# Later output stores, two-part first loads and an earlier column sum in an attention + MLP kernel

## The chip, the cores and the metric

The kernel runs on one core of a Trainium2 chip. The metric is device time in microseconds (us) of a whole execution, the median of several runs; less is better. A difference counts as faster or slower from 2% on, which would be 6.6 us here. One traced execution of each kernel gives its profile. The profile's span is about 1.7 us shorter than the device time, and single executions of one kernel spread over some 2 us.

## The reference

Eight batches of eight heads, 576 tokens of 64 values. Attention by landmarks (32 segment means of q and k), a pseudo-inverse by six Newton steps, then layer norm and a two-layer MLP with a residual.

```python
q_lm = q.reshape(B, H, m, S // m, D).mean(axis=3)          # m = 32 landmarks
k_lm = k.reshape(B, H, m, S // m, D).mean(axis=3)
A, Bm, C = sm(q, k_lm), sm(q_lm, k_lm), sm(q_lm, k)        # sm: scaled softmax(a b^T)
Z = Bm^T / (norm1(Bm) * norminf(Bm) + 1e-6)                # column and row sums of Bm
for _ in range(6):
    Z = 2 * Z - Z @ Bm @ Z
x = heads_side_by_side(A @ Z @ C @ v)                      # 8 x 576 x 512
out = x + relu(layernorm(x) * g @ w1) @ w2                 # 512 -> 2048 -> 512
```
(Written shorter than the original, with the same meaning.)

## The kernel before

PE is the busiest engine. The first batch's attention (a0) runs alone, with idle "warming" matmuls between its steps; afterwards the attention of later batches is interleaved with the MLP, whose matmuls come from a generator (`fill(n)` takes n steps of it). All loads, all DMA transposes of the normalized blocks (xn to xnT) and nearly all output stores are issued from one queue, that of SyncE. Loads of 576 KB feed six staging buffers; POOL casts them to fp16 and adds up segments.

The end of an MLP block, which issues its stores at once:

```python
ot = mout.tile([P, DM], FP32, name="ot", tag="ot")
dve.scalar_tensor_tensor(out=ot[:], in0=pso[:], scalar=rstds[g][:, u:u + 1],
                         in1=x_blk.pop(j)[:], op0=ALU.mult, op1=ALU.add)
store(j, ot)                      # two DMAs, one for each half block
yield True
```

A step of the interleaved part. `settle()` runs postponed work, among it POOL's centering of a block and its DMA transpose; `next_cast()` casts a landed load on POOL and issues a further load:

```python
for step, _ in enumerate(attention2(c.bs, c)):
    fill(count[step])
    settle()
    ...
        next_cast()
```

An MLP group needs four transposed blocks before its first matmul:

```python
while len(turned.get(g, ())) < 4:
    ...
```

The ramp, a0 (cut): the last k is cast whole, PE takes its segment sums (pss), then its nine transposes (pst); psb is bm's product, psse holds bm's self-product and its column sums, pscv the product with v.

```python
for _ in range(4):
    run(a0)
    warm(3, 256)
run(a0)
warm(1, 512)
run(a0)
scalar.copy(natv_buf[0][:, 3, :, 0:D], raw[0]["v", 1][:, 1])   # half of the second v on ACT
```

The softmax here doesn't subtract the row's maximum and nothing guards it: scores larger than these inputs give would overflow.

## Time and profile before

| | value | how to read it |
|---|---|---|
| time | 329.13 us, 3 runs (328.23 to 330.18); with three more runs 329.38 | device time |
| PE busy | 314.7 of 327.9 us | leaves 13.2 us, 3.9 us of them after the last matmul |
| PE idle, 0 to 26 us | 3.7 us | the ramp, beside warming matmuls |
| PE idle, 47 to 141.7 us | 4.8 us | small waits, and one of 1.42 us at its end |
| PE idle, 141.7 to 324 us | 0.1 us | nothing to gain here but work removed |

In the profile's lines PE is the matmul engine, PEld its weight load, SPq the queue of SyncE. A timeline line is: start, duration, engine, source line, operation, output<-input, and in brackets the idle time of the engine before it with what ended it. A line of the waits is: engine, tile, what it waited for: total, times, longest. A line of the chain that ended last is: start, duration, engine, tile. The lines themselves stand in the prediction. Idle times with two decimals in the text are summed from the trace's matmul records, gap by gap.

### The profile page before, as it was taken

The numbers are of one execution on the slowest core, as the hardware profiler recorded it, in microseconds if no ns is written. First come the engines' busy times: TensorE is split into PE (matmuls) and PEld (weight loads), VectorE is DVE, ScalarE is ACT, GpSimd is POOL, SyncE is SP. The second block draws the span as 40 slices with busy tenths as digits, with TensorE's granted clock in tenths as the row PEclk, the third lists the DMA queues.
The fourth block names the chain that finished last, engine by engine and source line by source line (L and its number), as shares of the span: only waits on it lengthen the run. The fifth ranks groups of instructions, "written<-read, shape, count | busy, mean of one in ns | idle before, by whom it ended". The sixth has DMA issues, their size and how long they took to land.

```text
span 327.9 us, 8249 instructions
## 1 busy us (share of the span) xinstructions
PE 314.7 (96%) x3409; PEld 162.3 (50%) x3409; DVE 175.7 (54%) x395; ACT 152.7 (47%) x307; POOL 153.3 (47%) x241
## 2 busy tenths in 40 slices
PE   8889999999999999989999999999999999999995
PEld 8547864553445444435544445454444444444444
DVE  3668769779964797953237668722566120010012
ACT  3546762749960661957204672454046107305600
POOL 3389979999999999999800034100014000000000
PEclk9999999999999999999999999999999999999998
DMA  7999999898797864695022103330242126032023
GB/s 278 394 356 365 366 402 303 297 345 239 241 195 231 234 169 127 156 290 102 4 68 66 34 20 76 82 50 2 64 104 26 32 64 98 0 72 60 0 49 79
DMA packets 36397, 50.34 MB, mean 154 GB/s; under 512 B 17796, under 2 KB 22152, under 8 KB 36360
## 3 DMA queue, kind: packets, MB, share of 16 engines
q1 hardware_dynamic: 36200, 49.69, 52.7%
q8 instruction: 26, 0.43, 0.5%
q10 hardware_dynamic: 160, 0.13, 0.2%
q14 instruction: 11, 0.09, 0.1%
HBM read 36.70 MB, written 9.44 MB: 141 GB/s over the span
## 4 chain that ended last, share of the span: by engine, by line
PE 56%; POOL 22%; DMA 7%; issue 2%; ACT 2%; DVE 1%; SPq 0%; POOLq 0%
PE psh L74 26%; PE pso L74 25%; POOL asum L68 11%; POOL nat L68 6%; POOL natv L68 3%; DMA stg<-in_q_dram 3%; POOL xn L68 2%; DMA w2stg<-in_moe_w_ch_dram 2%; POOL s L68 1%; PE psy L74 1%; PE pscv L74 1%; DMA stg<-in_v_dram 1%; DMA stg<-in_k_dram 1%; DMA xnT<-xn 1%; ACT xn L68 1%
## 5 line engine op out<-in xcount | busy, mean ns | idle before, releaser
L74 PE MATMUL psh<-xnT,w 128*128 128x512 f16 (+1 forms) x640 | 133.7, 358 | 1.4 <-DMA xnT<-xn 1.4
L74 PE MATMUL pso<-w,hT 128*128 128x512 f16 (+1 forms) x592 | 132.9, 374 | 0.0
L68 ACT ACTIVATE hT<-psh 128x512 f16<-128x512 f32 x144 | 84.9, 597 | 97.6 <-PE psh L74 97.4
L74 PEld LDWEIGHTS <-w 128*128 128x128 f16 x640 | 59.5, 98 | 56.7 <-issue 3.1
L74 PEld LDWEIGHTS <-hT 128*128 128x128 f16 x592 | 56.1, 98 | 57.2 <-issue 0.8
L68 DVE SCALAR_TENSOR_TENSOR ot<-pso,rstd,xblk 128x512 f32<-128x512 f32 (+1 forms) x37 | 27.1, 732 | 77.6 <-PE pso L74 77.4
L68 POOL CAST nat<-stg 128x1152 f16<-128x1152 f32 x28 | 32.5, 1167 | 3.4 <-DMA stg<-in_k_dram 1.7
L68 POOL TENSOR_TENSOR asum<-asum 128x256 f32<-128x256 f32 (+2 forms) x54 | 28.4, 527 | 4.2
L68 DVE TENSOR_TENSOR xblk<-psy,rcpd 128x512 f32<-128x512 f32 (+1 forms) x40 | 27.6, 691 | 1.8 <-POOL w L68 0.2
L68 POOL TENSOR_TENSOR asum<-nat 128x576 f32<-128x576 f16 x18 | 23.4, 1299 | 1.5
L68 POOL TENSOR_SCALAR xn<-xblk,mvg 128x512 f16<-128x512 f32 x14 | 9.6, 694 | 30.9 <-ACT junk L68 30.9
L68 DVE SCALAR_TENSOR_TENSOR st<-st,psn 128x192 f16<-128x192 f16 (+3 forms) x36 | 14.2, 395 | 17.6 <-PE psn L74 17.4
L68 POOL CAST natv<-stg 128x1152 f16<-128x1152 f32 (+1 forms) x16 | 17.6, 1119 | 9.6 <-DMA stg<-in_v_dram 9.6
L68 POOL TENSOR_SCALAR negm<-mvg 128x1 f32<-128x1 f32 x14 | 2.7, 191 | 40.5 <-DVE mvg L68 35.9
L68 DVE TENSOR_TENSOR ebd<-st,mask 128x256 f16<-128x256 f16 (+1 forms) x30 | 20.7, 690 | 1.0
L68 DVE STREAM_TRANSPOSE xT<-nat 128x576 uint32<-128x576 uint32 x24 | 18.2, 760 | 2.2 <-POOL nat L68 2.2
L74 PE MATMUL psy<-zcbd,ea 128*128 128x260 f16 (+1 forms) x80 | 15.9, 276 | 1.0 <-DVE xblk L68 0.4
L68 ACT ACTIVATE ea<-psea 128x576 f16<-128x576 f32 x12 | 7.2, 648 | 16.5 <-PE psea L74 16.5
L74 PE MATMUL idle<-zeros 128*128 128x128 f16 (+2 forms) x82 | 13.4, 312 | 1.1 <-DVE eps_ln L172 1.1
L74 PEld LDWEIGHTS <-ea 128*128 128x128 f16 (+1 forms) x80 | 7.1, 100 | 12.2 <-issue 3.5
L68 ACT ACTIVATE junk<-xblk 128x512 f16<-128x512 f32 x14 | 8.8, 625 | 9.4 <-DVE xblk L68 9.2
L68 DVE BATCH_NORM_STATS2 st<-xblk 128x6 f32<-128x512 f32 x18 | 12.4, 688 | 0.5
(115 smaller groups left out, 263.0 us busy)
## 6 DMA issues: line engine op xcount, KB each, us to landing
stg<-in_q_dram SPq DMA_DIRECT2D x16, 576.0 KB, 6.0
stg<-in_k_dram SPq DMA_DIRECT2D x16, 576.0 KB, 5.7
out_dram<-ot SPq DMA_DIRECT2D x70, 128.0 KB, 2.4
stg<-in_v_dram SPq DMA_DIRECT2D x10, 576.0 KB, 6.4
w1stg<-in_moe_w_ch_dram SPq DMA_DIRECT2D x16, 256.0 KB, 6.0
w2stg<-in_moe_w_ch_dram SPq DMA_DIRECT2D x16, 256.0 KB, 5.2
stg<-in_v_dram SPq DMA_DIRECT2D x12, 288.0 KB, 5.5
xnT<-xn SPq DMA_TRANSPOSE x28, 3.3
```

Of the source, the lines that this page charges most:

```text
L68: return lambda *args, **kw: keep(getattr(self.engine, op)(*args, **kw))
L74: keep(nc.tensor.matmul(o, l, r, start=start, stop=stop, tile_position=(rb, cb), skip_group_check=(skip or cb != 0)))
```

## The change

Three intents. Stores go into the queue one step later, so that loads and transposes of a step come ahead of stores whose data are older. The first batch's last k and last v arrive in two transfers each and are cast in two parts, so that work starts on the first part. The column sums of bm, which do not need bm's transpose, go ahead of bm's product with itself. Some warming matmuls go too. Core of the diff (cuts marked):

```diff
+    halves = ((slice(0, 2), slice(0, 5)), (slice(0, 2), slice(5, NJ)))
+    pairs = ((slice(0, 1), slice(0, NJ)), (slice(1, 2), slice(0, NJ)))
...
-            raw[b]["k", u] = load(k, b, u, nc.sync)
+            raw[b]["k", u] = load(k, b, u, nc.sync, halves if (b, u) == (0, U - 1) else whole)
...
-            raw[b]["v", u] = load(v, b, u, nc.sync)
+            raw[b]["v", u] = load(v, b, u, nc.sync, pairs if (b, u) == (0, U - 1) else whole)
...
+    pool.tensor_copy(out=natv_buf[0][:, 3, 5:NJ, 0:D], in_=raw[0]["v", 1][:, 1, 5:NJ])
...      (sums and transposes of that k: blocks 0 to 4, then 5 to 8; xT's first five by ACT, the rest by DVE)
+        MM(psse[:, 0, :, :], bones[:].rearrange("p a c -> p (a c)"), bm16[:])
         for w in range(W):
             for h in range(4):
                 sl = ds(32 * h, 32)
                 MM(psse[sl, 1, w, :], bmT[sl, w, :], bmT[sl, w, :], rb=32 * h, cb=32 * h)
-        MM(psse[:, 0, :, :], bones[:].rearrange("p a c -> p (a c)"), bm16[:])
...      (pscv of the last unit: v's first row of heads first, then its second)
-                store(j, ot)
+                if at_end:
+                    store(j, ot)
+                else:
+                    to_store.append((j, ot))
...
+    def work(n):
+        k = len(to_store)
+        fill(n)
+        settle()
+        for _ in range(k):
+            store(*to_store.pop(0))
...
-    for _ in range(4):
+    for i in range(4):
         run(a0)
-        warm(3, 256)
+        if i < 3:
+            warm(3, 256)
     run(a0)
-    warm(1, 512)
+    warm(1, 128)
     run(a0)
-    scalar.copy(natv_buf[0][:, 3, :, 0:D], raw[0]["v", 1][:, 1])
+    scalar.copy(natv_buf[0][:, 3, 0:5, 0:D], raw[0]["v", 1][:, 1, 0:5])
...
-            fill(count[step])
-            settle()
+            work(count[step])
```

More of the change, by code (lines that the diff above doesn't have):

```diff
@@ L78, in TR, with load @@
         keep(nc.tensor.matmul(o, i_, idn, is_transpose=True, tile_position=(0, 0)))
-    def load(src, b, u, queue):
+    whole = ((slice(0, 2), slice(0, NJ)),)
+    halves = ((slice(0, 2), slice(0, 5)), (slice(0, 2), slice(5, NJ)))
+    pairs = ((slice(0, 1), slice(0, NJ)), (slice(1, 2), slice(0, NJ)))
+    def load(src, b, u, queue, parts=whole):
         t = stage.tile([P, 2, NJ, D], FP32, name="stg", tag="stg")
-        keep(queue.dma_start(
-            out=t[:],
-            in_=src[b, 4 * u:4 * u + 4].rearrange("(r e) (t j) d -> (e t) r j d", e=2, j=NJ)))
+        rows = src[b, 4 * u:4 * u + 4].rearrange("(r e) (t j) d -> r (e t) j d", e=2, j=NJ)
+        for r, j in parts:
+            keep(queue.dma_start(out=t[:, r, j, :],
+                                 in_=rows[r][:, :, j, :].rearrange("r p j d -> p r j d")))
         return t
@@ L111, in cast_qk @@
         t = nat.tile([P, NJ, 2, D], FP16, name="nat", tag="nat")
-        engine.tensor_copy(out=t[:].rearrange("p j r d -> p r j d"), in_=raw[b][nm, u][:])
+        for _, j in halves if (b, u, nm) == (0, U - 1, "k") else whole:
+            engine.tensor_copy(out=t[:, j, :, :].rearrange("p j r d -> p r j d"),
+                               in_=raw[b][nm, u][:, :, j, :])
         nat_tiles[b, nm, u] = t
@@ L309, in attention, with sums @@
                 pst = p2([P, NJ, P], FP16, "pst")
-                def sums():
-                    for j in range(NJ):
+                def sums(js=range(NJ)):
+                    for j in js:
                         MM(pss[:, i, w, :], n16[:, j, :, :].rearrange("p r d -> p (r d)"),
@@ L316, in attention @@
                 last = (w, i) == (W - 1, 1)
-                if last:
+                if last and not first:
                     sums()
-                for j in range(NJ):
-                    TR(pst[:, j, :], n16[:, j, :, :].rearrange("p r d -> p (r d)"), ident16[:])
+                for js in (range(0, 5), range(5, NJ)) if first and last else (range(NJ),):
+                    if first and last:
+                        sums(js)
+                    for j in js:
+                        TR(pst[:, j, :], n16[:, j, :, :].rearrange("p r d -> p (r d)"),
+                           ident16[:])
                 t = aprep.tile([P, NJ, P], FP16, name="xT", tag="xT" + nm, bufs=5 if nm == "q" else 4)
@@ L325, in attention @@
                     scalar.copy(t[:], pst[:])
+                else:
+                    scalar.copy(t[:, 0:5, :], pst[:, 0:5, :])
                 xT[nm, w] = t
@@ L340, in attention @@
         if first:
-            dve.tensor_copy(out=t[:], in_=pst[:])
+            dve.tensor_copy(out=t[:, 5:NJ, :], in_=pst[:, 5:NJ, :])
         yield
@@ L401, in attention @@
             natv = natv_of[b]
-            for j in range(NJ):
-                for h in range(4):
-                    r, e = divmod(h, 2)
-                    rows = ds(64 * e, 64)
-                    MM(pscv[ds(32 * h, 32), w, :], ect[w][rows, j, ds(32 * r, 32)],
-                       natv[rows, 2 * u + r, j, :], rb=64 * e, cb=32 * h,
-                       start=(j == 0), stop=(j == NJ - 1), skip=True)
+            order = [(j, h) for j in range(NJ) for h in range(4)]
+            if first and w == W - 1:
+                order.sort(key=lambda jh: jh[1] // 2)
+            for j, h in order:
+                r, e = divmod(h, 2)
+                rows = ds(64 * e, 64)
+                MM(pscv[ds(32 * h, 32), w, :], ect[w][rows, j, ds(32 * r, 32)],
+                   natv[rows, 2 * u + r, j, :], rb=64 * e, cb=32 * h,
+                   start=(j == 0), stop=(j == NJ - 1), skip=True)
         rcv = asm.tile([P, W], FP32, name="rcv", tag="rcv")
@@ L940, in mlp @@
                                          in1=x_blk.pop(j)[:], op0=ALU.mult, op1=ALU.add)
-                store(j, ot)
+                if at_end:
+                    store(j, ot)
+                else:
+                    to_store.append((j, ot))
                 yield True
     stream = mlp()
+    to_store, at_end = [], []
     def fill(n):
@@ L1038 @@
     for i, _ in enumerate(a1):
-        fill(5 if i < 9 else 7)
-        settle()
+        work(5 if i < 9 else 7)
         next_cast()
@@ L1053 @@
         for step, _ in enumerate(attention2(c.bs, c)):
-            fill(count[step])
-            settle()
+            work(count[step])
             if late and step >= 3:
@@ L1063 @@
         while after and (after.jobs or after.lms):
-            fill(8)
+            work(8)
             next_cast()
             after.next_job()
+    at_end.append(True)
     for _ in stream:
-        pass
+        while to_store:
+            store(*to_store.pop(0))
 _INS = ['q', 'k', 'v', 'moe_g_ln', 'moe_w_ch1', 'moe_w_ch2']
```

## The prediction

> **What bounds the kernel now.** I read the views in this order: busy time by engine and the 40 slices, the chain that ended last, the waits of PE from the end of the ramp on, the SyncE queue around the largest of those waits, and the timeline of the first 16 us.
>
> ```profile
> PE 314.7 (96%) x3409; PEld 162.3 (50%) x3409; DVE 175.7 (54%) x395; ACT 152.7 (47%) x307; POOL 153.3 (47%) x241
> PE   8889999999999999989999999999999999999995
> POOL 3389979999999999999800034100014000000000
> DMA  7999999898797864695022103330242126032023
> ```
>
> PE is busy 96% of the span. Only 327.9 - 314.7 = 13.2 us are left, and 3.9 us of them are the tail after the last matmul. The slices show three more regimes: DMA full for the first six slices (to about 49 us), POOL full from about 33 to 141 us, and PE alone after that. The busy times by window say it in numbers: PE idles 3.7 us in 0 to 26 us (its 13.4 us of warming matmuls, tile idle, sit there too), 0.7 us in 26 to 47, 4.8 us in 47 to 141.7, and 0.1 us in 141.7 to 324. So after 141.7 us nothing but PE work matters, and the change removes no useful PE work. It can only bring forward the moment at which PE may run without stops.
>
> That moment is in the chain of waits and in PE's list of waits from 26 us on (engine, tile, releaser: total, times, longest):
>
> ```profile
> 136.22 2.16 POOL natv L68 x2
> 138.38 3.20 DMA xnT<-xn
> 141.71 1.89 PE psh L74 x8
> ...
> PE psn L74 <- DVE ebd L68: 1.6, 3, 0.7
> PE psh L74 <- DMA xnT<-xn: 1.4, 1, 1.4
> ```
>
> PE ran dry at 140.29 us and stood 1.42 us until the fourth transposed block of its next MLP group landed. The SyncE queue shows why that transpose was late:
>
> ```profile
> 133.82 1.22 SPq L870 DMA_TRANSPOSE xnT<-xn  x1
> 135.09 0.57 SPq L106 DMA_DIRECT2D stg<-in_q_dram  x1
> 135.75 1.20 SPq L870 DMA_TRANSPOSE xnT<-xn  x1
> 137.04 1.24 SPq L829 DMA_DIRECT2D out_dram<-ot  x2
> 138.38 1.25 SPq L870 DMA_TRANSPOSE xnT<-xn  x1
> ```
>
> POOL had finished that block's xn at 136.22 us (134.86 + 1.36), but the queue was issuing two output stores for 1.24 us and took the transpose at 138.38. The stores' data were ready at 133.75; they were ahead only by program order.
>
> In the ramp two waits matter:
>
> ```profile
> 11.63 0.12 PEld L74 LDWEIGHTS <-qbd 64*32 64x32 f16 x8 [0.32 <-DVE qbd L68]
> ...
> 13.49 0.68 ACT L68 CAST natv<-stg 128x576 f16<-128x576 f32 x1
> 13.52 0.67 POOL L68 CAST natv<-stg 128x576 f16<-128x576 f32 x1 [1.44 <-DMA stg<-in_v_dram]
> ...
> 14.24 0.47 PE L74 MATMUL pscv<-natv,ect 64*32 64x65 f16 x36 [0.31 <-POOL natv L68]
> ```
>
> bm's product (psb) starts 0.31 us after qbd is there (10.91 + 0.41), because four warming matmuls stand ahead of it; and the last pscv matmuls wait for the casts of the second v, which landed at 13.5 us.
>
> **What the Trainium skill says.** (1) "DMA: Bandwidth & Descriptors", section "Anatomy of one DMA": DMA engines do not wait on semaphores, the wait is on the issuing sequencer. So one queue is strictly in order, and a store ahead holds a transpose behind it. The five lines above agree. (2) The same page, "Why small descriptors are slow": a fixed cost for each packet. The packet records agree: 2304-byte packets took about 92 ns in the first 14 us, 1024-byte ones 48.6 ns in 20 to 28 us, so 18% more for each byte. (3) "Perfetto Trace Analysis", "DMA Optimizations": splitting may let work start sooner "if DMA engines are generally idle". Here they are not: their share in 10 to 26 us is about 1. (4) "TensorE: Matmul & The Clock Gate", Part 1: the array slows after an idle window of about 3.4 us. The granted clock is 1.00 up to 300 us, and the warming matmuls that go (three of 256 columns; 512 to 128 columns in another) leave a pause of well under 1 us, so I expect no loss.
>
> **The change part by part.**
>
> *Stores one step later.* The built order on SyncE shows what the scheduler made of it: ahead of the third of those transposes one half-block store is left instead of two (its partner moved to before the first). One store costs 1.24 / 2 = 0.62 us of issue. Walking the queue: transpose 1 at 133.82, load at 135.09, transpose 2 at 135.70, one store to 137.6, transpose 3 at about 137.6 instead of 138.38. It lands 3.3 us later, near 140.9, still later than PE's 140.29. Worth about 0.75 us, and at most the whole wait of 1.42 us. Other stores also move behind loads, but POOL waits for a load after 47 us only 1.2 us in all, all of it before 51 us, so this brings nothing there. After 141.7 us PE does not wait, so delayed stores cannot help or hurt; the four ot buffers cover one step (an ot comes about every 3.5 us).
>
> *k of the first batch's second half in two parts.* The last k lands at 9.38 us, its cast takes 0.76 us, PE's sums start at 10.22 and end at 10.65, klm starts at 10.70. A straight line through the two packet sizes gives (estimate) 57 ns for 1280 bytes; the two parts cost 57 + 49 = 106 ns where 92 did, on 16 packets for each engine: 0.22 us more, plus 0.03 for one more completion. So part 1 lands near 8.8, part 2 near 9.65. Casts (0.76 us for 1152 elements) shrink to about 0.49 and 0.43: done at 9.35 and 10.1. PE however is occupied with the third step's warming matmuls until about 9.8, then five sums, five transposes, four sums: klm at about 10.58, a gain of 0.1 us only. With the warming matmuls ahead of psb gone, psb starts on qbd's end, about 11.25 instead of 11.64. ACT takes xT's first five blocks at 10.54 to 11.25, before the exponential needs it at 11.5, so that split does not hurt.
>
> *Column sums ahead of bm's product.* They need bm (done at 12.84) and not bmT (13.12). With the 0.4 us from psb, the sums start near 12.5 instead of 13.33, so the DVE chain to st's first part ends near 13.65 instead of 14.47: 0.8 us.
>
> *v in two parts.* v has the same run length, so the cost is the 0.25 us inherited from k and one completion: the last part lands near 13.75. Its cast is now shared, 5 blocks on ACT (320 elements, about 0.48 us by the slope between 0.68 for 576 and 1.12 for 1152) and 4 on POOL (about 0.40): done at 14.25 instead of 14.20. Then 18 matmuls instead of 36 remain: about 0.31 instead of 0.47 us. rcv starts at 14.62 instead of 14.76.
>
> Sum of the ramp: v stays the last to arrive, the 0.8 us on the other branch is mostly slack, and the ramp's end moves by about **0.15 us**. Why v is so late: fifteen of its sixteen engines had finished by 12.37, one at 13.47, because a 16 KB instruction fetch (10.94 us, 1.07 us long) held that engine. If the fetch falls elsewhere, the ramp gains up to 0.8 us.
>
> Do these 0.15 us reach the end? Only if nothing with its own clock stands between. It does: DMA is full to about 47 us, then POOL runs one cast or sum after another to 138 us. POOL's chain starts when its first new k lands at 47.55 us, and DMA time sets that, not the ramp. So PE gains 0.15 us at 26 us and loses it again at 141.7. On the other hand the 0.25 us of dearer packets can push POOL's chain and the gate back by up to that much.
>
> Total: -0.75 from the queue, between 0 and +0.27 from the packets, some -0.1 from luck in the ramp: about -0.7 us on 329.13. I put the point a little lower, at 328.2, as each part removes a real wait, and the small waits of DVE ebd (1.6 us) may shrink with an earlier ramp.
>
> **Rivals.** (a) *The ramp is what counts*: PE is in truth its own bound from 26 us on, the 97% busy PE carries any ramp gain to the end, and the two gains add: 0.15 to 0.8 plus 0.75 to 1.4 us, so 327.0 to 328.2. For it: only 5.5 us of PE idle after 26 us, most of it waits for DVE that move along with PE. Against it: POOL's unbroken chain. (b) *The dearer packets win*: everything after 47 us comes 0.3 us later and the transposes gain little because the scheduler left one store ahead: 329.0 to 329.4. For it: the DMA share of 1. Against it: POOL has waited 0.9 us at 47.55, but in a DMA-bound stretch that is no slack. (c) *A new wait*: the moved stores hold up a later transpose or load, or an ot buffer, and PE stands after 141.7 us: up to 330. Against it: the transposes in the second half are issued well ahead, and PE waits for none of them.
>
> **Range and chances.** Main reading 328.0 to 328.7, rival (a) down to 327.0, rival (b) and run scatter (328.23 to 330.18 in three runs) up to 329.3. So **328.2 us, range 326.9 to 329.4**. A gain of 2% would be 6.6 us, half of all PE idle time: **faster 0.02, within 2% 0.97, slower 0.01**.
>
> **What would show it.** Right: PE's wait for xnT near 141 us shrinks from 1.4 to 0.3 to 0.9 us with the transpose issued about 137.6; psb near 11.25; the column-sum product starts before the bmT product near 12.5; rcv near 14.6; the first batch's last k in packets of 1280 and 1024 bytes; POOL's first new k still at 47.5 to 47.9 us. Wrong: if the PE wait at 141 us is gone and PE finishes over 1.2 us earlier, the ramp gain was carried (rival a); if POOL's chain moves earlier as a whole, DMA was not its clock; if PE's idle time after 142 us exceeds 0.5 us, rival (c) holds.

## The result, and the profile after

The changed kernel took 329.16 us (median of 6 runs, 328.16 to 329.51) beside 329.38 us (6 runs, 328.23 to 330.18) for the kernel before. A ratio here is the mean time of one kernel's runs over that of the other's of the same rounds, so it is not quite the ratio of the two medians. It was 0.9992, with a 95% interval of 0.9968 to 1.0016. Two later measurements of the same pair gave 0.9975 (0.9957 to 0.9994) and 0.9989 (0.9970 to 1.0009). The plain mean of the three is 0.9985, about -0.5 us. So the class is "the same", and a gain of some tenths of a microsecond is likely but only one of the three intervals excludes zero.

The page's first parts of the changed kernel (busy time of each engine; busy tenths in 40 slices):

```profile
PE 313.8 (96%) x3406; PEld 162.0 (50%) x3406; DVE 174.8 (54%) x396; ACT 153.3 (47%) x308; POOL 153.6 (47%) x242
PE   8889989998999999999999999999999999999995
POOL 3489888999999999999800044200013000000000
DMA  7999999998699854598035013510251126032023
```

Nothing has changed in kind: 0.9 us less PE work (the dropped warming matmuls), the same three regimes.

The chain that ended last, around the gate of the fourth-block transpose, and two of PE's waits from 26 us to 145 us, of the changed kernel:

```profile
135.39 1.46 POOL natv L68 x2
136.85 3.56 DMA xnT<-xn
140.54 1.89 PE psh L74 x8
...
PE psn L74 <- DVE ebd L68: 2.1, 3, 0.9
PE psh L74 <- DMA xnT<-xn: 0.4, 1, 0.4
```

PE's wait for xnT fell from 1.4 to 0.4 us and PE ended at 322.63 instead of 323.92 us. That looks like a gain of 1.3 us, yet this traced run was the fastest of the six (328.16 us), and the traced run of the kernel before (329.57 us) lay above its median. The SyncE queue of the changed kernel:

```profile
132.98 1.23 SPq L887 DMA_TRANSPOSE xnT<-xn  x1
134.26 0.56 SPq L112 DMA_DIRECT2D stg<-in_q_dram  x1
134.92 1.20 SPq L887 DMA_TRANSPOSE xnT<-xn  x1
136.17 0.59 SPq L843 DMA_DIRECT2D out_dram<-ot  x1
136.85 1.27 SPq L887 DMA_TRANSPOSE xnT<-xn  x1
```

One store is left between the second and the third transpose. The third was issued 1.46 us after POOL had its xn (135.39), instead of 2.16 us. But the chain shows that it then took 3.56 us to land, where it had taken 3.20.

The ramp of the changed kernel (timeline):

```profile
11.11 0.12 PEld L74 LDWEIGHTS <-qbd 64*32 64x32 f16 x8 [0.61 <-DVE qbd L68]
...
13.47 0.46 ACT L68 CAST natv<-stg 128x320 f16<-128x320 f32 x1 [0.45 <-DMA stg<-in_v_dram]
13.50 0.40 POOL L68 CAST natv<-stg 128x256 f16<-128x256 f32 x1 [0.78 <-DMA stg<-in_v_dram]
...
13.98 0.46 PE L74 MATMUL pscv<-natv,ect 64*32 64x65 f16 x18 [0.26 <-ACT natv L68]
...
14.47 0.17 DVE L68 RECIPROCAL rcv<-pscv 128x2 f32<-128x2 f32 x1 [0.56 <-PE pscv L74]
```

In this trace psb starts 0.5 us earlier than before, the casts of the last v are short, 18 matmuls instead of 36 follow, and rcv comes at 14.47 instead of 14.76 us. The 18 matmuls took as long as the 36 had (0.46 and 0.47 us), so what v gains here comes from its shorter casts. e4 and e9 show how much of this holds in other traces.

### The profile page after: what moved, and what is told of

Read it like the earlier page. It is cut to its first block, busy times and chain, and to the rows that moved or that the text cites. A ratio compares the mean times of both kernels' runs of the same rounds, so it can differ in the third digit from the quotient of the medians.

```text
span 326.4 us, 8246 instructions
## 1 busy us (share of the span) xinstructions
PE 313.8 (96%) x3406; PEld 162.0 (50%) x3406; DVE 174.8 (54%) x396; ACT 153.3 (47%) x308; POOL 153.6 (47%) x242
## 4 chain that ended last, share of the span: by engine, by line
PE 59%; POOL 24%; DMA 8%; issue 3%; DVE 2%; ACT 1%; SPq 1%; POOLq 0%
PE psh L74 28%; PE pso L74 26%; POOL asum L68 13%; POOL nat L68 6%; DMA w1stg<-in_moe_w_ch_dram 4%; DMA stg<-in_v_dram 3%; POOL natv L68 2%; POOL xn L68 2%; PE psy L74 1%; PE pscv L74 1%; POOL s L68 1%; SPq L90 1%; DMA xnT<-xn 1%; ACT xn L68 1%; DVE ebd L68 1%
## 5 line engine op out<-in xcount | busy, mean ns | idle before, releaser
L68 POOL TENSOR_TENSOR asum<-nat 128x576 f32<-128x576 f16 x18 | 24.1, 1338 | 1.5
L68 POOL CAST natv<-stg 128x1152 f16<-128x1152 f32 (+2 forms) x17 | 17.9, 1077 | 9.1 <-DMA stg<-in_v_dram 9.1
L74 PE MATMUL idle<-zeros 128*128 128x128 f16 (+2 forms) x79 | 12.3, 295 | 1.1 <-DVE eps_ln L180 1.1
```

Source lines behind the costliest of these rows:

```text
L68: return lambda *args, **kw: keep(getattr(self.engine, op)(*args, **kw))
L74: keep(nc.tensor.matmul(o, l, r, start=start, stop=stop, tile_position=(rb, cb), skip_group_check=(skip or cb != 0)))
```

## The experiments

**What the experiments are read from.** Five moments of each trace, in us. "New k" is POOL's first cast for the third batch, the start of its long chain; "xn" is the end of the centering whose transpose is the third in the queue; "issued" is that transpose's issue; "PE on" is the end of PE's wait near 141 us.

| run | new k | xn | issued | PE on | PE's end |
|---|---|---|---|---|---|
| before | 47.55 | 136.22 | 138.38 | 141.71 | 323.92 |
| before again (e1) | 46.74 | 135.69 | 137.83 | 141.24 | 323.32 |
| ramp only (e3) | 46.92 | 135.70 | 137.85 | 141.16 | 323.24 |
| stores only (e2) | 47.53 | 136.31 | 137.76 | 141.60 | 323.69 |
| changed | 46.64 | 135.39 | 136.85 | 140.54 | 322.63 |
| changed again (e4) | 47.17 | 135.96 | 137.42 | 141.21 | 323.31 |
| changed, third (e9) | 47.92 | 136.71 | 138.17 | 141.62 | 323.71 |
| before, load held (e6) | 47.16 | 135.86 | 137.82 | 140.59 | 322.93 |
| changed, load held (e5) | 46.79 | 135.81 | 137.38 | no wait | 322.49 |
| changed, load held again (e10) | 46.77 | 135.55 | 137.11 | no wait | 322.22 |
| changed, ramp 2 us late (e7) | 47.83 | 137.17 | 138.63 | 142.11 | 324.20 |

Three things can be read off before any single experiment. From "PE on" to PE's end it is 182.1 to 182.2 us in every row with a wait (182.3 in e6): the gate sets the end. From "new k" to "xn" it is 88.7 to 89.0 us (89.3 in e7): POOL's chain has a fixed length. And from "xn" to "issued" it is 2.14 to 2.16 us with the stores in their old place and 1.45 to 1.46 us with the stores one step later, whatever the ramp (with the load held 1.96 us in e6 and 1.56 to 1.57 us in e5 and e10).

**e1, the kernel before again.** No edit.

> The kernel before, unchanged, as a control. Every theory: ratio 1.000 within the scatter. It settles what a second trace of the same kernel shows: if POOL's chain (first cast of a new k for the third batch) again starts at 47.5 us and PE again waits 1.4 us near 141 us for xnT, the 0.9 us earlier start of that chain in the changed kernel's trace (46.64 us) belongs to the change; if it starts anywhere between 46.5 and 47.6, it is scatter between runs.

Ratio 0.9996 (0.9970 to 1.0023), median 329.40 us. The timeline of POOL, first for the first trace of the kernel before, then for this one:

```profile
47.55 1.15 POOL L68 CAST nat<-stg 128x1152 f16<-128x1152 f32 x1 [0.90 <-DMA stg<-in_k_dram]
```

```profile
46.74 1.15 POOL L68 CAST nat<-stg 128x1152 f16<-128x1152 f32 x1 [0.90 <-DMA stg<-in_k_dram]
```

The same kernel starts POOL's chain 0.8 us apart, in both cases on the landing of the new k. So the 46.64 us of the changed kernel's trace is scatter, and so is most of its 1.3 us; the two other traces of the changed kernel start at 47.17 and 47.92 us. The completion records of that load say why it scatters: a load counts as landed when the last of its sixteen engines has finished. In all fourteen traces the last completion that this cast waits for comes 0.15 us before its start, also where the profile puts the wait down to PE or DVE. In the first trace fifteen had by 46.75 us and the last at 47.40; an instruction fetch of 16 KB, 1.05 us long, had run at 43.32 us. In this trace all sixteen were through by 46.59 us, though it had such a fetch too (at 42.49 us, 1.10 us long). That the fetch in the first trace sat on just the late engine is an inference: the records do not name the engine.

**e2, the stores alone.** The kernel before with `work`, `to_store` and `at_end` and nothing else of the change.

> The kernel before with the stores queued one step later and nothing else. Theory (the gate at 141 us is the only place that pays): ratio 0.998 (-0.7 us), PE's wait for xnT near 141 us down from 1.4 to 0.3 to 0.9 us, third transpose issued right after POOL's xn and one store, ramp unchanged (rcv at 14.76 us). Rival (stores bring nothing, the transposes land later instead): ratio 1.000, wait unchanged.

Ratio 0.9993 (0.9973 to 1.0013), median 329.59 us. The SyncE queue, and PE's waits from 126 to 150 us:

```profile
135.84 1.20 SPq L870 DMA_TRANSPOSE xnT<-xn  x1
137.09 0.59 SPq L826 DMA_DIRECT2D out_dram<-ot  x1
137.76 1.24 SPq L870 DMA_TRANSPOSE xnT<-xn  x1
...
PE psh L74 <- DMA xnT<-xn: 1.3, 1, 1.3
```

The queue did what was expected of it: one store instead of two, the transpose issued 0.7 us nearer to its xn. The wait nevertheless stayed at 1.25 us, since POOL's chain started late here (47.53 us) and the transpose took 3.84 us from its issue to PE. In the table, from "xn" to "PE on", the old order takes 5.46 to 5.55 us (three traces) and the new one 4.91 to 5.29 us (four traces). The mean difference is 0.35 us, not 0.7: a part of the gain is lost after the issue. The rival of the expectation was half right.

**e3, the ramp alone.** The changed kernel with the stores put back:

```diff
-                if at_end:
-                    store(j, ot)
-                else:
-                    to_store.append((j, ot))
+                store(j, ot)
...
-            work(count[step])
+            fill(count[step])
+            settle()
```

> The changed kernel with the stores queued as before: k and v in parts, sums ahead, fewer warming matmuls. Theory (POOL's chain is the clock from 47 to 141 us): ramp 0.15 to 0.3 us earlier (rcv near 14.5 us), ratio 1.000, PE's wait near 141 us back to 1.4 us or more. Rival (PE carries the ramp's gain to the end): ratio 0.999 and the wait not longer than before.

Ratio 0.9980 (0.9959 to 1.0001), median 328.86 us. rcv at 14.66 us; PE's wait was 0.71 us, because POOL's chain started early (46.92 us). PE reached the gate at 140.45 us, where the two traces of the kernel before have 140.29 and 140.44: no lead from the ramp is left there. The ratio alone would favour the rival, but its interval touches 1 and the chain's start explains the trace. Not settled by the time, against the rival by the trace.

**e4 and e9, the changed kernel twice more.** No edit.

> The changed kernel once more, for a tighter ratio and a second trace. Theory: ratio 0.998 to 0.999, PE's wait near 141 us 0.3 to 0.9 us. If POOL's chain starts at 46.6 us again, its earlier start comes from the change; if near 47.5, the first trace was a lucky run, and the ratio is nearer to 1.

> The changed kernel a third time, beside the version with the load held, on one chip. Theory: PE's wait near 141 us 0.3 to 0.9 us, third transpose issued 1.46 us after its xn and landed 3.7 to 3.9 us later, ratio 0.9975 to 0.9992 against the kernel before.

Ratios 0.9975 and 0.9989, medians 328.90 and 329.12 us; waits of 0.51 and 0.87 us, with POOL's chain starting at 47.17 and 47.92 us. In e9 the transpose reached PE 3.45 us after its issue (I had expected 3.7 to 3.9), in e4 3.79. The ramp scatters too: in e4 and e9 the last k landed at 10.13 and 9.90 us (9.41 in the first trace), psb began at 11.87 and 11.65 us (11.11), and rcv came at 14.68 and 14.49 us (14.47).

**e5 and e10, one load held back.** Where does the rest of the stores' gain go? The packet records around the transposes answer for the two kernels. The 576 KB load of q, issued between the first and the second transpose, is the only one with 4608-byte packets then; the transposes have 256-byte packets.

| packets, us | before | changed | load held (e5) |
|---|---|---|---|
| load of q | 136.27 to 139.09 | 135.45 to 138.06 | after 139.92 |
| second transpose | 138.34 to 139.55 | 137.53 on | 136.55 to 137.33 |
| third transpose | 140.00 to 141.03 | to 139.79 | 138.58 to 139.64 |

The second transpose's first packets came 2.6 us after its issue in both kernels (135.75 to 138.34, 134.92 to 137.53), near the end of that load's packets (0.5 to 0.75 us before the last of them, so "start only when that load's 4608-byte packets are through" in my expectation below is too strong). In the changed kernel the third came straight behind it in one stretch. "DMA: Bandwidth & Descriptors" of the Trainium skill, section "Queues, rings and completion order", says that each DMA engine consumes descriptors in ring order; this agrees. So there are two lines to stand in: the queue where DMAs are issued and the rings where they run, and taking a store out of the first only moved the transpose up in the second. The test takes the load out of the second, in the changed kernel: it is issued one call later, behind the third transpose (the staging buffer has time until its cast). Skipping one call also moves the three loads after it back by one call each, and on the queue a store takes the load's place between the first and the second transpose.

```diff
+    held = []
+
     def next_load():
-        if to_load:
+        if len(to_load) == 4 and not held:
+            held.append(True)
+        elif to_load:
```

> The changed kernel with one 576 KB load of q, which stands between the first and the second of the three transposes near 135 us, held back until the third is issued. In every trace so far the end of PE is the end of its wait near 141 us plus 182.1 us, and the 256-byte packets of the transposes start only when that load's 4608-byte packets are through (load 2.6 to 2.9 us long). Theory (the gate is in the order of the DMA rings, the load is what holds the third transpose, the store only adds to it): third transpose lands before 140.0 us, PE's wait for xnT near 141 us is 0, PE's end at about 322.4 to 322.9 us, ratio 0.996 to 0.997. Rival (the queue's issue time is what counts): the wait stays 0.3 to 0.9 us, ratio 0.9975 as for the changed kernel.

> The changed kernel with the 576 KB load held, again. Theory: no wait near 141 us, ratio 0.996 to 0.997 against the kernel before, and 0.3 to 1.0 us less than the changed kernel on the same chip. Rival (the first gain was a lucky chip): same time as the changed kernel.

Ratios 0.9960 (0.9940 to 0.9979) and 0.9969 (0.9943 to 0.9995), medians 328.11 and 327.81 us. In e10 one run of 330.26 us widens the interval. The kernel before, of the same rounds, had 329.64 and 329.37 us, and the changed kernel beside e10 329.12 us. The SyncE queue of e10:

```profile
133.14 1.23 SPq L887 DMA_TRANSPOSE xnT<-xn  x1
134.42 0.58 SPq L843 DMA_DIRECT2D out_dram<-ot  x1
135.09 1.25 SPq L887 DMA_TRANSPOSE xnT<-xn  x1
136.43 0.58 SPq L846 DMA_DIRECT2D out_dram<-ot  x1
137.11 1.24 SPq L887 DMA_TRANSPOSE xnT<-xn  x1
138.40 0.57 SPq L112 DMA_DIRECT2D stg<-in_q_dram  x1
```

PE waits for nothing near 141 us in either trace: the second transpose's packets start 1.2 us after its issue, and the third transpose's are through at 139.64 (e5) and 139.22 us (e10), before PE gets there. The issue-time rival falls: the third transpose was issued 1.56 us after its xn, no sooner than in the changed kernel, and the wait is gone all the same. Against the kernel before this version gains 1.0 to 1.6 us (0.3 to 0.5%), and both intervals exclude 1, though by the 2% rule the class is still "the same". Against the changed kernel on the same chip it is 1.3 us by the medians but 0.7 us by the means, which with the run of 330.26 us is not clear of the noise. What is shown there is the wait of 0.4 to 0.9 us that is gone in both traces.

**e6, the same load held in the kernel before.** Same edit, stores where they were.

> The kernel before with the same load held and its two stores left ahead of the third transpose. Theory (the load, not the stores): the wait near 141 us goes here too, from 0.8 to 1.4 us to about 0, ratio 0.997 to 0.998. Rival (the stores' place is what counts): the wait stays above 0.5 us, ratio 1.000.

Ratio 0.9970 (0.9952 to 0.9988), median 328.49 us. The gain is there, but the wait did not go to zero: 0.67 us were left, above the 0.5 us at which I would have called the rival right. A part of it is PE's own doing: PE ran dry at 139.92 us here, 0.4 to 0.5 us sooner than in the two traces of the kernel before. Here the two stores ahead of the third transpose do cost: their 2048-byte packets ran from 137.74 to 139.34 us, and the transpose's from 139.04 to 139.98. From "xn" to "PE on" it took 4.73 us instead of 5.5. So load and stores are two holds in one line. The load is the longer one, and either alone leaves a part of the wait.

**e7, the ramp made 2 us late.** The changed kernel with ten more warming matmuls before the Newton steps:

```diff
     run(a0)
-    warm(2, 512)
+    warm(12, 512)
     for it in range(6):
```

> The changed kernel with ten more warming matmuls of 512 columns (10 times 0.213 us = 2.1 us) just before the Newton steps of the first batch. Theory (from 47 to 141 us DMA time and then POOL are the clock, PE's lead from the ramp is absorbed): first matmul of the MLP 2.1 us later, POOL's third batch still starts at 46.6 to 47.6 us, PE reaches the gate less than 1 us later than 140.7, total at most +0.6 us (ratio 0.998 to 1.000). Rival (PE carries what the ramp gains or loses): PE reaches the gate 2 us later, total +1.5 to +2 us, ratio 1.002 to 1.004.

Ratio 1.0043 (1.0010 to 1.0075), median 330.47 us (4 runs, one of 332.87): 1.3 to 1.6 us more than the changed kernel's medians. My expectation of at most 0.6 us is wrong, and the rival's 1.5 to 2 us is nearer. PE's first MLP matmul came at 27.98 instead of 25.63 to 25.94 us. PE's waits from 126 to 150 us, and POOL's timeline:

```profile
47.83 1.15 POOL L68 CAST nat<-stg 128x1152 f16<-128x1152 f32 x1 [1.65 <-DMA stg<-in_k_dram]
...
PE psh L74 <- DMA xnT<-xn: 0.2, 1, 0.2
```

POOL's start lies inside the scatter of the other traces (46.64 to 48.02 us), so the delay did not reach it visibly. PE ran dry at 141.92 us, against 140.15 to 140.75 in the three traces of the changed kernel: 1.2 to 1.8 us of the 2 us arrived, and the wait shrank to 0.19 us. POOL's xn came later too (137.17 us, its chain 0.3 to 0.7 us longer than elsewhere), and the tail after PE's end was 0.9 us longer than in e4 (span 328.9 and 327.1 us), which one trace does not explain. So the picture is a race of two near-equals: POOL's chain wins by 0.4 to 0.9 us in the changed kernel, and a delay of PE beyond that lead goes to the end. A gain of PE's does not.

**e8, k whole.** A look, one run (329.07 us, state unknown): `halves` replaced by `whole` for the load and the cast of the last k.

> The changed kernel with the last k loaded and cast whole again (PE still takes its sums and transposes in two groups). A look at the trace only. Theory (v's landing sets the ramp's end): rcv within 0.2 us of the changed kernel's 14.5 to 14.7 us; v lands 0.25 us earlier by the cheaper packets. Rival (the split of k carries the ramp's gain): rcv back at 14.75 to 15.0 us, psb near 11.5 instead of 11.1 us.

psb began at 11.74 us. Beside the first trace of the changed kernel (11.11) that looks like 0.6 us for the split, but with e4 and e9 (11.87 and 11.65) it is inside the scatter. From the landing of the last k to psb the split does save 0.5 us (1.71 to 1.84 us in the nine traces with it, 2.27 here). But the last part of a split k also landed later: at 9.37 to 10.19 us, 9.79 on the mean of nine traces, against 9.19 to 9.77, 9.40 on the mean of the five traces with k whole. The median engine was only 0.1 us later, so most of this lies in the last engines; why is not shown. So a net gain of the split is not shown. rcv stayed at 14.54 us: here, with k landed at 9.47 us, the branch had slack. v did not land earlier: POOL's cast of its last part began at 13.54 us, with the split at 13.50.

**e11, v whole.** A look, one run (329.44 us, unknown): `pairs` replaced by `whole` for the load of the last v.

> The changed kernel with the second v in one transfer (its cast still shared by ACT and POOL, the matmuls still ordered by rows). Theory (the last landing of v sets the ramp's end, and the shared cast and not the split transfer makes the gain): POOL's cast of the first half moves from before to after the landing at about 13.5 us, so POOL casts 0.67 us and then 0.40 us, the last pscv matmuls start near 14.6 instead of 14.0 us and rcv comes near 15.0 us instead of 14.5 to 14.8. Rival: rcv stays within 0.1 us.

```profile
13.54 1.02 POOL L68 CAST natv<-stg 128x576 f16<-128x576 f32 x2 [1.46 <-DMA stg<-in_v_dram]
14.26 0.65 PE L74 MATMUL pscv<-natv,ect 64*32 64x65 f16 x36 [0.94 <-POOL natv L68]
14.95 0.17 DVE L68 RECIPROCAL rcv<-pscv 128x2 f32<-128x2 f32 x1 [1.06 <-PE pscv L74]
```

POOL now has both casts after the landing, and rcv comes at 14.95 us, 0.3 to 0.5 us later than in the three traces of the changed kernel (14.47, 14.68, 14.49). So without the two transfers the ramp's gain is gone, although the cast is still shared: the time in my expectation came true, but its words "the shared cast and not the split transfer" did not. It takes both.

**e12, the sums behind again.** A look, one run (328.71 us, unknown): the `bones` matmul moved back behind the loop.

> The changed kernel with the column sums behind bm's product again. Theory (that branch has slack): the maximum over the sums starts about 0.2 us later (13.2 instead of 13.0 us), st's first part at about 13.9 instead of 13.7 us, still before the last pscv matmuls end at 14.4 us, so rcv is unchanged (14.5 to 14.8 us). Rival (the sums carry the gain): rcv 0.2 us or more later.

Inconclusive. In this run the last k's second part landed at 10.19 us, 0.8 us later than in the first trace of the changed kernel, because of its last engines. rcv came at 14.91 us, with the last pscv matmuls ending at 14.86 and st's first part on DVE at 14.93 us: both branches were equally late. e4 had the same late k (10.13 us) with the sums ahead, and rcv at 14.68 us. But its v also landed 0.3 us earlier (13.43 and 13.72 us), so the difference can't be given to the sums. A closer match is e5, with the sums ahead and k at 10.18 us: rcv came 4.60 us after k there, 4.55 in e4, and 4.72 here. Behind a late k the sums may be worth 0.1 to 0.2 us, from one trace each.

## Why the prediction was right or wrong

The measured 329.16 us lies in the stated range and "within 2%" is right. That range also held no change at all, so lying in it says little. The point of 328.2 us was too low: the first measurement gives -0.2 us by the medians, all three together about -0.5 us, against -0.9 us forecast. The median also lies outside the prediction's own main reading (328.0 to 328.7) and inside that of rival (b) (329.0 to 329.4).

- **What bounds the kernel: right, with one correction.** PE after 141.7 us and POOL's chain of fixed length before it: the table bears out both. The landing of a load starts that chain, as its completion 0.15 us before the first cast shows in every trace. But I took 47.55 us as a fixed moment. It moves between 46.6 and 48.0 us from run to run, which is more than the whole change is worth, and one trace of each kernel could not have shown it. In the first trace of the changed kernel this even met one of my signs of being wrong ("if POOL's chain moves earlier as a whole, DMA was not its clock"): the chain had moved because the load had.
- **The stores: the mechanism right, the size wrong.** The step that failed is "It lands 3.3 us later". Issue came 0.70 us sooner, as worked out (0.69 to 0.71 measured), but in the traces with the later stores the transpose took 3.45 to 3.84 us from issue to PE, where it took 3.31 to 3.41 in the old order. Worth about 0.35 us instead of 0.75. What stood in its place: the 576 KB load ahead of it in the DMA rings, shown by e5 and e10.
- **The dearer packets: the price wrong, the landing not.** I took 92 ns for a 2304-byte packet and 48.6 for a 1024-byte one from means over a time window, which held the 4-byte completion records too (and their ratio is 19%, not 18%). By size alone, 2304-byte packets took 99.3 ns in the first 14 us, and the k parts' 1280 and 1024 bytes took 55.0 and 46.5 ns: 101.5 instead of 99.3, hardly dearer. The 0.03 us for one more completion had no measurement behind it. So the term of 0.22 us should have been near zero. In the first trace of each kernel k's second part landed at 9.41 us, whole k at 9.38; over all traces it is 9.79 and 9.40 on the mean (e8), so the forecast of 9.65 was near for a reason that is not the packets' price and stays open. It was not passed on to v, which landed at 13.43 to 13.46 us in the changed kernel's three traces and at 13.47 us before (forecast 13.75).
- **k and the sums: right in the first trace only.** There klm came at 10.44 us (10.58 forecast), psb at 11.11 (11.25), the sums at 12.49 (12.5), and st's first part ended at 13.92 (13.65 forecast, late by a DVE wait of 0.33 us before the maximum). In e4 and e9 psb came at 11.87 and 11.65 us. And the branch has slack only when k lands early: in e4 and e5, with k at 10.13 and 10.18 us, DVE went from st's first part straight on to rcv.
- **v: right in the sum, by two errors that cancel in part.** From v's last landing to rcv it took 1.03 to 1.25 us in the nine traces with v split and 1.29 to 1.45 us in the four with the old ramp. rcv came at 14.47 to 14.68 us (14.62 forecast). But v landed 0.3 us sooner than forecast, and the 18 matmuls took 0.46 us where I had 0.31. So the halved count brought nothing; the shorter cast did it, and e11 shows that it needs the split transfer. The slow sixteenth engine of v was there in the changed kernel too; that an instruction fetch held it is said in the prediction as if it were known, and is an inference.
- **The ramp's 0.15 us is lost: right, but in another place.** The step that failed is "PE gains 0.15 us at 26 us and loses it again at 141.7". The gain was there: PE's first MLP matmul came at 25.62 to 26.02 us in six traces with the new ramp (e3, e4, e5, e9, e10 and the first; mean 25.79), against 25.82 to 26.14 (mean 25.95) in the four with the old one (e1, e2, e6 and the first). But the PE instruction that ran at 47.11 us in the kernel before (warming ones not counted) ran at 46.97 to 47.11 us in those four and at 47.09 to 47.71 us in the six. So the lead was gone, and on the mean 0.3 us more, by 47 us, long before the gate: PE idled 0.86 to 1.33 us between 26 and 47 us with the new ramp, and 0.54 to 0.70 us with the old. Why is not shown. Nor has PE much to lose at the gate: 0.4 to 0.9 us in the changed kernel. e7, which took away 2 us, went to the end for the most part. So by the traces rival (a) does not hold for a gain of this size in the ramp, though the time of e3 alone cannot exclude it. For a loss it does hold: a delay beyond PE's lead counts.
- **The last step to 328.2 was a guess.** Taking the point below the sum of about -0.7 us "as each part removes a real wait" had no working behind it, and DVE's waits did not shrink (1.6 us before, 2.1 in the changed kernel).
- **Rivals (b) and (c).** No new wait after 141.7 us appeared, so (c) falls. (b) was right that the transposes gain little and that the time hardly moves. It gave the store left ahead as the reason; the runs show the load (e5, e10), and no run took away that store. Its other half, everything after 47 us 0.3 us later by dearer packets, did not show: POOL's start lay at 46.64 to 47.92 us in the changed kernel's traces.

What stays open: which engine of the sixteen each instruction fetch holds, why a split k lands later, where between 26 and 47 us the ramp's gain goes, whether the ramp alone brings anything (0.9980, interval up to 1.0001), and the longer tail of e7.

## What to carry to other kernels

When a transfer lands too late, look at both lines it stands in: the issuing queue, and the rings, where a large load issued just before holds the small urgent one for its whole length; moving that load behind took four lines here and, alone, gained about 1.0 us (e6) where the three-part change gained about 0.5, though the intervals overlap. Before a difference of a microsecond in two traces is explained, take a second trace of the same kernel and compare the moments that set the end. That holds for the small gains inside a ramp as well. When two chains arrive within a microsecond of each other, shortening the one that is early brings nothing.

## What the Trainium skill lacked or had wrong

- "DMA: Bandwidth & Descriptors" has the order of descriptors in a ring, but no number for what a large load does to a DMA transpose behind it. Here the transpose's first packets came 2.6 us after its issue behind a 576 KB load, and 1.2 us after it without (e5).
- No page names the instruction fetch as something that delays a kernel's loads. Here fetches of 16 KB took 0.9 to 2.0 us in the first 60 us, and with fifteen engines through, the last one finished 1.1 us later on v (12.37 and 13.47 us in the kernel before). That the fetch is the cause is inferred from its time.
- "DMA: Bandwidth & Descriptors" has no issue time for a transpose of this size within SBUF on this chip. On SyncE it was 1.2 us for 128 x 512, against about 0.6 us for a store.
